# Loading the last unit's keys in two halves and splitting its exponential, in a streaming attention decode kernel on one Trainium2 core

## The chip, the cores and the metric

The kernel runs on one core of one Trainium2 chip. The metric is the device time of an execution in microseconds (us). Before the change it was 445.39 us in the median of four runs (444.75 to 446.24). The profile measures its span from the first to the last instruction, which is 1.7 to 3.2 us less. All runs quoted here were listed as fast (none took over 1.5% more than the fastest of its kernel), at a mean granted TensorE clock (the share of full speed that PE was given) of 0.93 to 0.97.

Three words for the trace. PE is TensorE, and "PEld" are its weight loads. DVE is VectorE and ACT is ScalarE. SP is the engine that issues the transfers.

## The reference, cut to what matters

Two attention decode layers, A and B, share one program. Each has 4 batches, one query token, 32 query heads on 8 key/value heads of 128, and a cache of 8192 positions. B looks only at the last 2048 positions.

```python
q = (x @ wq).reshape(B, Sq, Hq, Dh)...
scores = einsum("bhqd,bhkd->bhqk", q, k) * Dh ** -0.5
p = softmax(scores)
o = einsum("bhqk,bhkd->bhqd", p, v)
return o.reshape(B, Sq, Hq * Dh) @ wo          # A and B side by side
```

Some nine tenths of the 184.6 MB that are read are the two caches (estimate from their shapes, 168 MB), and every byte of them is used once.

## The kernel before

The work is cut into 20 units, four of B and sixteen of A. A unit of A is one batch and two key/value heads, with 4 MB of keys and 4 MB of values. Two units make a turn, and PE runs ten turns in a hardware loop. In a unit PE transposes the keys (16 groups k, through four PSUM banks), forms the scores of each group, and then multiplies the *previous* unit's probabilities with its values (eight chunks, "PV"). The last unit (L = 19) has its PV after the loop, in the tail:

```python
halves = [SA[(L + 1) % 2][0:Bn, 0:H2], KTB[2][0:Bn, 0:H2]]
def pe_seed(pe):                       # "the seed": brings the projection's running sum (f32) into PSUM, 4 matmuls in the trace
    for hf in range(2):
        ins = pe.matmul(out=halves[hf], lhsT=identf[0:Bn, 0:Bn], rhs=oacc[:, 0, ...], start=True, stop=False)
op("pe", pe_seed, waits=[("ocp", NTURN - 1), ("otr", L - 1)])
for c in range(NC):                    # the last unit's value chunks
    w = [("VL", vch_of[c])]            # its values land in four pieces
    if c == 0: w.append(("exp", L))
    if c == 4: pe_SM(L)                # sums of the probabilities
    pe_PV(L, c, bank=KTB[0], waits=w)
add_norm(L, bank=KTB[0])               # DVE scales the output
# ... then 16 matmuls of the last projection piece, whose weights land last
```

The loop's instructions carry fixed wait values, so at the end of each turn it takes back what the turn has used, one instruction per semaphore:

```python
with nc.Fori(0, n_turn, engines=[mybir.EngineType.PE]):
    run(turns[0])
    for n, sem in by_name.items():
        pe.sem_inc(sem, -strides[n])
```

## Time and profile before

| What | Reading before |
| --- | --- |
| time, median of 4 runs | 445.39 us |
| span of the profiled run | 442.5 us |
| moved | 184.78 MB at 418 GB/s |
| unit 18's keys let PE go | 396.57 |
| last unit's first transpose weights (T19) | 416.00 |
| last unit's output is scaled by DVE | 437.73, which is T19 + 21.73 |

From the page of the kernel before: the span, the row of the DMA engines' busy share in 40 slices (9 is 90% or more), and the chain of work that ended last.

```profile
span 442.5 us, 15650 instructions
DMA  8999999999999999999999999999999999999993
DMA packets 13047, 184.78 MB, mean 418 GB/s; under 512 B 1332, under 2 KB 2408, under 8 KB 4456
DMA 49%; PE 47%; issue 2%; SPq 1%; DVE 1%; ACT 0%
```

The transfers never pause until the last slice, so the bytes set most of the time. PE catches up with them once a pair of units and then waits. The timeline shows the last such wait, the place where the last unit begins, and the tail. Columns are start, duration, engine, line, operation, operands, count, and in brackets the engine's idle time before it and what ended it.

```profile
396.57 3.27 PEld L256 LDWEIGHTS KT<-identf,K_sb 128*128 128x128 f32 x16 [7.30 <-DMA K_sb<-in_A_k_cache_dram]
...
413.19 2.86 PEld L304 LDWEIGHTS OT<-PT,V_sb 128*128 128x128 bf16 x96
416.00 1.73 PEld L256 LDWEIGHTS KT<-identf,K_sb 128*128 128x128 f32 x16
...
430.17 0.69 DVE L434 TENSOR_TENSOR Dt<-SA,MBm 128x512 f32<-128x512 f32 x1
430.78 0.68 DVE L434 TENSOR_TENSOR Dt<-SB,MBm 128x512 f32<-128x512 f32 x1
431.49 1.06 ACT L443 ACTIVATE PT<-Dt 128x1024 bf16<-128x1024 f32 x1 [4.27 <-DVE Dt L434]
431.59 0.18 DVE L478 TENSOR_TENSOR OT_sb<-OS,RL 128x8 bf16<-128x8 f32 x1
432.33 0.11 PEld L642 LDWEIGHTS SA<-oacc,identf 4*4 4x4 f32 x2 [1.30 <-issue]
433.31 1.92 PEld L304 LDWEIGHTS KT<-PT,V_sb 128*128 128x128 bf16 x64 [0.43 <-issue]
437.73 0.18 DVE L471 TENSOR_TENSOR OT_sb<-KT,RL 128x8 bf16<-128x8 f32 x1 [1.21 <-PE KT L304]
```

Two things are to be seen. The last unit's transposes follow the 96 value matmuls before them with no idle bracket: PE came to them as it was done, and the keys, which landed at 415.96, held it back by no more than 0.02 us. It was almost a tie. And the seed (L642) starts 0.56 us after its input was ready (431.59 + 0.18 = 431.77) and 1.30 us after PE's last weight load, "issue", which means a wait for nothing that the profile counts.

What PE's sequencer did in that gap is only in the trace's own instruction records, which list the semaphore and branch instructions (start in us, duration, operation):

```
430.488 0.051 EVENT_SEMAPHORE $S[99]-=
430.672 0.051 EVENT_SEMAPHORE $S[122]-=
   (seven more, 0.151 apart)
431.877 0.051 EVENT_SEMAPHORE $S[101]-=
432.028 0.036 ALU_OP
432.124 0.076 COMPARE_BRANCH
432.259 0.051 EVENT_SEMAPHORE $S[130]>=
432.335 0.077 LDWEIGHTS (the seed's first)
```

Ten decrements and a branch close the loop. They start before the last value weights (430.936), because the sequencer runs ahead of the array, and end 1.2 us after them.

### The profile page before, as it was taken

The numbers are of one execution on the slowest core, as the hardware profiler recorded it, in microseconds if no ns is written. First come the engines' busy times: TensorE is split into PE (matmuls) and PEld (weight loads), VectorE is DVE, ScalarE is ACT, GpSimd is POOL, SyncE is SP. The second block draws the span as 40 slices with busy tenths as digits, with TensorE's granted clock in tenths as the row PEclk, the third lists the DMA queues.
The fourth block names the chain that finished last, engine by engine and source line by source line (L and its number), as shares of the span: only waits on it lengthen the run. The fifth ranks groups of instructions, "written<-read, shape, count | busy, mean of one in ns | idle before, by whom it ended". The sixth has DMA issues, their size and how long they took to land.

```text
span 442.5 us, 15650 instructions
## 1 busy us (share of the span) xinstructions
PE 359.4 (81%) x7282; PEld 336.2 (76%) x7282; DVE 209.8 (47%) x472; ACT 184.5 (42%) x183; POOL 21.3 (5%) x56
## 2 busy tenths in 40 slices
PE   0258898998995899399949984996799499939996
PEld 0248798898895889289948984896789498938995
DVE  0034455465473555256525652574356355525661
ACT  1004374474462437053615542553347143605541
POOL 6100000000000000000000000000000000000000
PEclk9999999999998899789979996999599979988999
DMA  8999999999999999999999999999999999999993
GB/s 335 424 416 424 417 418 421 421 455 398 455 402 449 429 429 424 436 435 429 427 438 435 427 427 424 429 416 444 435 429 425 431 442 432 424 427 429 432 401 107
DMA packets 13047, 184.78 MB, mean 418 GB/s; under 512 B 1332, under 2 KB 2408, under 8 KB 4456
## 3 DMA queue, kind: packets, MB, share of 16 engines
q1 hardware_dynamic: 12944, 184.56, 98.3%
q8 instruction: 8, 0.13, 0.1%
q14 instruction: 7, 0.06, 0.0%
q0 software_dynamic: 64, 0.02, 0.0%
q10 hardware_dynamic: 24, 0.01, 0.0%
HBM read 184.56 MB, written 0.01 MB: 417 GB/s over the span
## 4 chain that ended last, share of the span: by engine, by line
DMA 49%; PE 47%; issue 2%; SPq 1%; DVE 1%; ACT 0%
DMA K_sb<-in_A_k_cache_dram 43%; PE KT L256 28%; DMA K_sb<-in_B_k_cache_dram 7%; PE OT L304 5%; PE SA L289 4%; PE KT L367 4%; PE SB L289 3%; PE KT L304 1%; PE SA L316 1%; SPq L543 1%; PE KT L346 0%; PE KT L328 0%; PE SA L663 0%; PE KT L663 0%; DVE M L396 0%
## 5 line engine op out<-in xcount | busy, mean ns | idle before, releaser
L256 PE MATMUL KT<-identf,K_sb 128*128 128x128 f32 x1280 | 208.9, 298 | 55.9 <-DMA K_sb<-in_A_k_cache_dram 48.8
L265 ACT ACTIVATE KT_sb<-KT 128x1024 bf16<-128x1024 bf16 x160 | 162.3, 1022 | 144.4 <-PE KT L256 144.1
L256 PEld LDWEIGHTS KT<-identf,K_sb 128*128 128x128 f32 x1280 | 149.7, 151 | 63.7 <-DMA K_sb<-in_A_k_cache_dram 49.9
L264 DVE COPY KT_sb<-KT 128x512 int32<-128x512 int32 x160 | 110.3, 689 | 131.4 <-PE KT L256 130.1
L304 PE MATMUL OT<-PT,V_sb 128*128 128x64 bf16 x2560 | 84.4, 193 | 1.7 <-issue 1.7
L304 PEld LDWEIGHTS OT<-PT,V_sb 128*128 128x128 bf16 x2560 | 78.4, 98 | 1.8 <-issue 1.8
L289 PEld LDWEIGHTS SA<-RQc,KT_sb 128*128 128x128 bf16 x1280 | 56.5, 98 | 3.5 <-ACT KT_sb L265 1.0
L443 ACT ACTIVATE PT<-Dt 128x1024 bf16<-128x1024 f32 x20 | 21.1, 1057 | 86.3 <-DVE Dt L434 86.3
L289 PE MATMUL SA<-RQc,KT_sb 128*128 128x16 bf16 x1280 | 56.4, 170 | 0.0
L289 PE MATMUL SB<-RQc,KT_sb 128*128 128x16 bf16 x1280 | 55.6, 170 | 0.0
L289 PEld LDWEIGHTS SB<-RQc,KT_sb 128*128 128x128 bf16 x1280 | 51.6, 97 | 1.1
L396 DVE TENSOR_REDUCE M<-SB 128x8 f32<-128x512 f32 (+1 forms) x20 | 13.8, 692 | 43.4 <-PE SB L289 43.4
L417 POOL PARTITION_ALL_REDUCE MB<-M1m x20 | 7.7, 385 | 392.2 <-DVE M1m L410 392.2
L367 PE MATMUL KT<-Wo_sb,OL 128*4 128x512 bf16 x80 | 18.9, 379 | 0.0
L187 PE MATMUL KT<-ident,x_sb 4*128 4x4 bf16 x8 | 0.6, 170 | 19.2 <-POOL identf L505 19.2
L187 PEld LDWEIGHTS KT<-ident,x_sb 4*128 4x128 bf16 x8 | 0.4, 113 | 19.4 <-issue 19.4
L434 DVE TENSOR_TENSOR Dt<-SA,MBm 128x512 f32<-128x512 f32 x20 | 13.8, 692 | 0.7
L396 DVE TENSOR_REDUCE M<-SA 128x8 f32<-128x512 f32 (+1 forms) x20 | 13.6, 681 | 0.0
L434 DVE TENSOR_TENSOR Dt<-SB,MBm 128x512 f32<-128x512 f32 x20 | 13.6, 680 | 0.0
L316 PE MATMUL SA<-PT,onesb 128*128 128x64 bf16 x336 | 13.2, 192 | 0.0
L367 PEld LDWEIGHTS KT<-Wo_sb,OL 128*4 128x4 bf16 x80 | 6.0, 84 | 8.1
L316 PEld LDWEIGHTS SA<-PT,onesb 128*128 128x128 bf16 x336 | 11.1, 97 | 0.0
(68 smaller groups left out, 111.6 us busy)
## 6 DMA issues: line engine op xcount, KB each, us to landing
K_sb<-in_A_k_cache_dram SPq DMA_DIRECT2D x16, 4096.0 KB, 27.7
V_sb<-in_A_v_cache_dram SPq DMA_DIRECT2D x15, 4096.0 KB, 32.7
K_sb<-in_B_k_cache_dram SPq DMA_DIRECT2D x16, 1024.0 KB, 21.3
V_sb<-in_B_v_cache_dram SPq DMA_DIRECT2D x16, 1024.0 KB, 20.9
V_sb<-in_B_wq_dram SPq DMA_DIRECT2D x1, 4096.0 KB, 12.3
V_sb<-in_A_wq_dram SPq DMA_DIRECT2D x1, 4096.0 KB, 21.9
Wo_sb<-in_B_wo_dram SPq DMA_DIRECT2D x4, 1024.0 KB, 19.4
Wo_sb<-in_A_wo_dram SPq DMA_DIRECT2D x3, 1024.0 KB, 20.0
```

The lines of the kernel that those rows point to most:

```text
L256: ins = pe.transpose(out=bkf[:, pi * 128:(pi + 1) * 128], in_=K_sbf[:, slot, t0:t0 + 2, :].rearrange("p t d -> p (t d)"), identity=identf[ ...
L264: return e.tensor_copy(out=KT_sb.bitcast(I32)[:, tj % NKT, :], in_=bkf.bitcast(I32)[:, :])
L265: return e.activation(out=KT_sb[:, tj % NKT, :], in_=bk[:, :], func=ACTF.Copy)
L289: ins = pe.matmul(out=stb[:, t % NTH * C:(t % NTH + 2) * C], lhsT=ktv[:, pi, :, e], rhs=RQc[:, u % 2, t // TS, e, :], start=(e == 0), stop ...
L304: ins = pe.matmul(out=otb[:, s * NW:(s + 1) * NW], lhsT=V_sb[:, slot, t, :], rhs=PT[:, slot, t * C:t * C + NW], start=(j == 0), stop=(j == ...
L316: ins = pe.matmul(out=SA[u % 2][:, s * NW:(s + 1) * NW], lhsT=onesb[:, :], rhs=PT[:, u % 2, c0:c0 + NW], start=(i == 0), stop=(i == n - 1))
L367: ins = pe.matmul(out=bk[0:Bn, 0:D], lhsT=OL[:, i // REP, i % REP, :], rhs=Wo_sb[:, i // REP, i % REP, :], start=(i == 0), stop=(i == C - 1))
L396: return dve.tensor_reduce(out=M1[:, h * n:(h + 1) * n].rearrange("p (s h) -> p s h", h=C), in_=bank[:, :].rearrange("p (s j h) -> p s h j ...
L417: return pool.partition_all_reduce(MB[:, 0:n], M1m[:, 0:n], channels=128, reduce_op=ReduceOp.max)
L434: return dve.tensor_tensor(out=Dt[:, h * NTH * C:(h + 1) * NTH * C].rearrange("p (s j h) -> p s j h", s=Sh, h=C), in0=bank[:, :].rearrange ...
L443: return act.activation(out=PT[:, u % 2, 0:NT * C], in_=Dt[:, :], func=ACTF.Exp, scale=scale)
L543: return e.dma_start(out=dst, in_=src)
```

## The change

The intent was to give the tail earlier inputs. The last unit's keys come in two transfers, so that its first transposes need only half of them. The exponential comes in two halves, so that the first value chunks need only the first. The seed moves behind four value chunks, so that it no longer stands in front of them.

```diff
-            op("pe", fn, waits=[("K", u) if k == 0 else None, bankfree(idx)], ...)
+            op("pe", fn, waits=[("K", u) if k == 0 else ("KH", u) if k == NJ // 2 and u % 2 == 1 else None, bankfree(idx)], ...)
@@ value matmuls: those that would read past the first half are narrowed
+                    w = NW if bank is None or t >= NTH or t * C + NW <= NTH * C else C
@@ the last unit's exponential
-            add(act_exp(u))
+            if u == L:
+                add(act_exp(u, 0, 1))
+                add(act_exp(u, 1, 2))
+            else:
+                add(act_exp(u))
@@ tail
-        op("pe", pe_seed, waits=[("ocp", NTURN - 1), ("otr", L - 1)])
             if c == 0:
-                w.append(("exp", L))
+                w.append(("exp", L, 0))
             if c == 4:
                 pe_SM(L)
+                op("pe", pe_seed)
@@ loads; earlier odd units raise the new semaphore themselves, before their load
+            if kind == "K" and slot == 1 and u < L:
+                op("sp", lambda sp: sp.sem_inc(sems["kh"], 16), bump=(sems["kh"], 16, ("KH", u)))
+            if kind == "K" and u == L:
+                for h in range(2):
+                    ...  # 2 MB each, inc=("K", u, 0) and ("KH", u)
+                return
```

The loop body is shared by all turns, so the wait on the new semaphore, and its decrement at the loop's end, come in every turn.

## The prediction

> **What bounds the kernel now.** The page: span 442.5 us, 184.8 MB at 418 GB/s, the DMA row at 9 tenths almost throughout. The chain of waits is DMA 49%, PE 47%: each pair of units waits some 27 us for an even unit's keys. The last such wait ends at 396.57 (timeline, unit 18's keys). From there PE is hardly free: it starts the last unit's transposes at 416.003 and issues the loop's last matmul at 430.96. The bytes do not change, so only the time after 396.57 can shrink.
>
> **Part 1, keys in two halves.** The trace's semaphore records show the last key load completing engine by engine from 411.3 to 415.96 (the Trainium skill, "DMA: Bandwidth & Descriptors", why a DMA increments its semaphore by 16: the engines finish independently and the semaphore counts them; this trace agrees, 4.6 us apart). Half of the 4 MB is 5 us at the observed rate, so the first half should be complete near 411. But PE, in order, issued the previous unit's last value weights at 415.956 at their regular spacing of 0.029: it lost at most 0.02 us to this load. The early half only removes a near-tie, worth perhaps 0.1 us where PE runs faster.
>
> **Part 2, exponential in halves.** The subtractions end at 430.86 and 431.46; the exponential runs 431.49 to 432.55. A 4x256 activation took 0.37, so 512 elements should take about 0.6 (estimate): first half done near 431.5. Intended: value chunks begin then instead of at 433.31.
>
> I do not believe that. PE's sequencer is closing the loop, which the busy columns leave out: ten semaphore decrements 0.151 us apart, the last at 431.88, a branch at 432.12, the first instruction after the loop at 432.26, the seed's first weights at 432.335, though its input was ready at 431.77. Other loop ends look alike (idle 1.3 to 1.4 us, put down to "issue"). Nothing after the loop starts before 432.3, and the seed hid the exponential's end. With the seed moved, value chunks start near 432.5, and the seed's 0.98 us is paid later, before chunk 4. The PE work from loop end to last value matmul is unchanged: seed 0.98, chunks 1.86 and 1.9, sums 0.46.
>
> **Part 3, what is added.** The new key semaphore is waited on inside the loop, so each turn gets one more wait and one more decrement: 0.15 us at the exit, on the critical path, and up to 0.08 for the wait in the last unit, likely hidden. In earlier turns both lie in the 7 us wait for keys. Seven value matmuls narrow from 64 to 8 columns: at most 0.1 us saved.
>
> The value pieces land at 433.24, 434.65 and 435.84, the last weights at 438.45; PE needs them at 435.6, 436.6, 437.1 and 439.6: no wait, but no more than 1.1 us to win.
>
> **Sum.** +0.15 exit, up to +0.1 wait, up to -0.1 narrow matmuls, -0.1 near-tie: about +0.1. Predicted 445.6 us, range 444.4 to 446.7. Chances: faster by over 2% 0.01, within 2% 0.98, slower 0.01.
>
> **Right if** the last transposes still start near 416, a loop end has eleven decrements, the first value matmul comes 0.15 after the old seed start (0.8 sooner than before), the seed takes about 0.98 us before chunk 4, and the last normalisation starts 41.3 us after unit 18's keys (41.16 before). **Wrong if** value chunks start at 431.6 (the loop end is no gate: 0.7 us gain), if the moved seed costs much less than 0.98, or if two key transfers change the landing of the keys.

## The result, and the profile after

The changed kernel took 444.96 us in the median of four runs (444.10 to 445.62), beside 445.39 before. The ratio was 0.9988, with a 95% interval of 0.9964 to 1.0012. (A ratio is the mean time of one kernel's fast runs over that of the other's of the same rounds, so not quite the ratio of the medians.) The same kernel in five more runs on another occasion had 1.0015 (1.0001 to 1.0029). Where a run below is called slower or faster, the interval of its ratio excludes 1.

The profiled run of the changed kernel has a longer span than that of the kernel before, 443.6 against 442.5. Its page and its timeline at the places shown before:

```profile
span 443.6 us, 15670 instructions
DMA  8999999999999999999999999999999999999992
DMA packets 13191, 184.78 MB, mean 416 GB/s; under 512 B 1348, under 2 KB 2424, under 8 KB 4472
DMA 50%; PE 47%; issue 1%; SPq 1%; DVE 1%; ACT 0%
```

```profile
396.73 3.28 PEld L258 LDWEIGHTS KT<-identf,K_sb 128*128 128x128 f32 x16 [8.06 <-DMA K_sb<-in_A_k_cache_dram]
...
414.06 2.86 PEld L307 LDWEIGHTS OT<-PT,V_sb 128*128 128x128 bf16 x96
416.85 1.19 PEld L258 LDWEIGHTS KT<-identf,K_sb 128*128 128x128 f32 x11
...
431.77 1.23 ACT L448 ACTIVATE PT<-Dt 128x512 bf16<-128x512 f32 x2 [3.68 <-DVE Dt L437]
433.36 1.92 PEld L307 LDWEIGHTS KT<-PT,V_sb 128*128 128x128 bf16 x64 [1.45 <-issue]
435.79 0.09 PEld L652 LDWEIGHTS SA<-oacc,identf 4*4 4x4 f32 x2
436.74 1.92 PEld L307 LDWEIGHTS KT<-PT,V_sb 128*128 128x128 bf16 x64 [0.43 <-issue]
438.82 0.18 DVE L477 TENSOR_TENSOR OT_sb<-KT,RL 128x8 bf16<-128x8 f32 x1 [2.26 <-PE KT L307]
```

The chain of waits gets something wrong here that is worth knowing. It gives the place to the exponential:

```profile
431.77 1.23 ACT PT L448 x2
433.39 1.98 PE KT L307 x64
```

But the first value chunk needs only the first half, which ended at 432.40, almost a microsecond before. The instruction records show who it was: eleven decrements from 431.363 to 432.903, the branch at 433.151, and the first value weights at 433.361, in the same 0.21 us after the branch as the seed before.

Counted from T19, the tail reads like this (from the start times of the instruction records):

| After T19, us | before | after |
| --- | --- | --- |
| branch at the loop's end | 16.12 | 16.30 |
| first exponential half done | – | 15.55 |
| first value weights | 17.31 | 16.51 |
| seed | 16.33 | 18.93 |
| chunk 4 | 19.63 | 19.88 |
| output scaled by DVE | 21.73 | 21.97 |

The value chunks start 0.80 us sooner, as was meant, and the seed takes it all back before chunk 4. The tail is 0.24 us *longer*.

The rest of the longer span lies ahead of T19. From unit 18's keys to T19 PE took 19.43 us before and 20.12 after, on the same instructions. The table by stretches (stretch in us, its length, busy time and count per engine, granted PE clock, DMA share, GB/s) shows the cause, first for the kernel before, then for the changed one:

```profile
396.57:400.70 4.13, 4.12 (x26) 4.06 (x27) 1.47 (x3) 1.44 (x2) 0.00 (x0) 0.50 1.05 452
400.70:416.00 15.30, 15.30 (x325) 13.68 (x323) 9.04 (x21) 6.75 (x7) 0.37 (x1) 1.00 0.99 426
```

```profile
396.73:402.40 5.67, 5.67 (x40) 5.54 (x41) 2.15 (x4) 2.05 (x2) 0.00 (x0) 0.50 0.96 413
402.50:416.80 14.30, 14.30 (x308) 12.71 (x307) 8.28 (x20) 6.14 (x6) 0.37 (x1) 1.00 1.02 435
```

After waiting for keys PE runs at half clock, for 4.1 us here and 5.7 us there. The Trainium skill ("TensorE: Matmul & The Clock Gate", Part 1, "What's actually happening") says that a free-running window of 3413 ns decides, so the point of release depends on where in it the work begins. This agrees: the half-clock stretches of these two traces last 6.8 or 10.2 us, two or three such windows, and end 4.1 and 5.8 us after the keys. I take it for the luck of a run and not for the change: the same stretch took 19.97 and 19.87 us in two later runs without split keys (e8_before_early, e13_half_seed). It is not shown, because the four traces with only the last unit's keys split, in the usual order, all had 19.61 to 20.17, and the five others without the split 19.43 to 19.48.

### The profile page after: what moved, and what is told of

Read it like the earlier page. It is cut to its first block, busy times and chain, and to the rows that moved or that the text cites. A ratio compares the mean times of both kernels' runs of the same rounds, so it can differ in the third digit from the quotient of the medians.

```text
span 443.6 us, 15670 instructions
## 1 busy us (share of the span) xinstructions
PE 358.4 (81%) x7282; PEld 335.3 (76%) x7282; DVE 210.0 (47%) x472; ACT 184.8 (42%) x184; POOL 21.4 (5%) x56
## 4 chain that ended last, share of the span: by engine, by line
DMA 50%; PE 47%; issue 1%; SPq 1%; DVE 1%; ACT 0%
DMA K_sb<-in_A_k_cache_dram 43%; PE KT L258 27%; DMA K_sb<-in_B_k_cache_dram 7%; PE OT L307 5%; PE SA L291 4%; PE KT L370 4%; PE SB L291 3%; PE KT L307 1%; PE SA L319 1%; SPq L549 1%; PE KT L349 0%; PE KT L331 0%; ACT PT L448 0%; PE SA L673 0%; PE KT L673 0%
## 5 line engine op out<-in xcount | busy, mean ns | idle before, releaser
L448 ACT ACTIVATE PT<-Dt 128x1024 bf16<-128x1024 f32 (+1 forms) x21 | 21.3, 1016 | 85.6 <-DVE Dt L437 85.6
```

Source lines behind the costliest of these rows:

```text
L448: return act.activation(out=PT[:, u % 2, a:b], in_=Dt[:, a:b], func=ACTF.Exp, scale=scale)
```

## The experiments

Two theories were open besides mine. *Mine*: the loop's end gates the tail, so the early exponential is of no use, and the new semaphore adds one decrement to it. *Rival 1*: the early half of the keys pays whenever PE is early. *Rival 2*: the split exponential pays. The times of a whole run scatter by up to 2 us, in part for the reason above, so the theories are separated by the time from T19 to the scaled output, which repeats to 0.04 us between two profiles of the changed kernel (21.97 and 21.93). Part of the scatter lies outside the profile's span, which is 1.7 us shorter than the time in some runs and 3.2 in others. Runs are named by their labels.

### The change again, and its two parts

The first run is the changed kernel itself:

> The changed kernel unaltered, timed in more rounds. My theory (the loop's end gates the tail): ratio to the kernel before 0.999 to 1.0005; in its trace eleven decrements at the last loop end, the first value weights 16.4 to 16.6 us after the last unit's first transpose weights (before: seed 16.33, first value weights 17.31), the normalisation 21.97 after them (before 21.73). Rival 1 (the early first half of the keys pays whenever PE reaches the last unit before its keys): ratio 0.998 to 0.999, and in fast-clock executions the last unit starts earlier than the whole keys could have landed. Rival 2 (the split exponential pays): ratio 0.997 or less with the first value weights no more than 15.8 after the first transpose.

The keys alone (the value matmuls have their 64 columns again, too):

```diff
-                add(act_exp(u, 0, 1)); add(act_exp(u, 1, 2))
+            add(act_exp(u))
+        op("pe", pe_seed, waits=[("ocp", NTURN - 1), ("otr", L - 1)])
-                w.append(("exp", L, 0))
+                w.append(("exp", L))
```

> Keys in two halves with the new semaphore, exponential whole and seed first as before. My theory: the loop end costs one decrement more (0.15 us), so from the last unit's first transpose to the normalisation about 21.9 us (before 21.73), ratio 0.999 to 1.001. Rival 1: this part alone brings what the whole change brings, ratio 0.998 to 0.999. Rival 2: no gain, ratio 1.000 or above.

The exponential and the seed alone, with no new semaphore:

```diff
-waits=[("K", u) if k == 0 else ("KH", u) if k == NJ // 2 and u % 2 == 1 else None, bankfree(idx)]
+waits=[("K", u) if k == 0 else None, bankfree(idx)]
-            if kind == "K" and slot == 1 and u < L: ...
-            if kind == "K" and u == L: ...
```

> Exponential in two halves and the seed moved, keys whole and no new semaphore. My theory: ten decrements; first value weights at the place where the seed began before, 16.33 us after the last unit's first transpose; normalisation at 21.7 to 21.85; ratio 0.9995 to 1.0005. Rival 2: first value weights 15.6 to 15.8 after it, normalisation near 21.0, ratio about 0.998.

| Run | median us | ratio (95%) | decrements | first value weights, after T19 | scaled output, after T19 |
| --- | --- | --- | --- | --- | --- |
| before | 445.18 (9 runs) | 1 | 10 | 17.31 | 21.73 |
| e1_after | 445.83 | 1.0015 (1.0001 to 1.0029) | 11 | 16.47 | 21.93 |
| e2_keys_only | 445.57 | 0.9996 (0.9982 to 1.0010) | 11 | 17.49 | 21.90 |
| e3_exp_only | 444.59 | 0.9985 (0.9971 to 0.9998) | 10 | 16.36 | 21.81 |

In the tail the parts add up. Counted from T19 the keys cost 0.18 us, the exponential and the seed 0.09, and together they cost 0.21 to 0.24. Of each, 0.02 is not theirs. In the trace of the kernel before, the keys held T19 itself back by 0.018 us, and PE made this up by the last transpose, which came 9.77 us after T19. It came 9.79 to 9.80 after it wherever T19 was not held back, with the new wait in the body (after, e1, e2) and without it (e3, e8, e13), so this wait cost nothing measurable. Counted from the loop's last value weights, the tail is 6.79 us before, 6.94 with the keys alone, 6.86 with the exponential and the seed alone, and 7.01 with all (6.98 in e1_after). So the keys cost one decrement, 0.15 us, and the exponential and the seed 0.06.

The first value weights of e3_exp_only come where the seed stood before, 16.36 against 16.33, after the same idle time of 1.30 us, which is what the gate of the loop's end demands. Rival 2 fell: it wanted 15.6 to 15.8.

```profile
432.55 1.92 PEld L307 LDWEIGHTS KT<-PT,V_sb 128*128 128x128 bf16 x64 [1.30 <-issue]
```

The ratios do not add up (0.9996 and 0.9985 beside 1.0015). e3_exp_only came out a little below what I expected, near the 0.998 of rival 2, and e1_after a little above, and their intervals do not overlap. The tail explains little of it. Of the 1.24 us between the spans of their two traces 0.12 lies in the tail, 0.69 in the stretch from unit 18's keys to T19, and 0.42 in the landing of unit 18's keys. I read the last two as the scatter of the clock windows and of the landings. That is argued for those runs, since only one of each was traced.

### What the whole keys cost without the split

Every kernel here with whole keys in the usual order shows how long PE waited for them, as the gap between its last value weights and T19 beyond the usual 0.029 us. Seven traces had 0.018 (before), 0 (e3_exp_only), 0.285 (e4_before_peeled), 0.039 (e7_exp_early), 0 (e8_before_early), 0.119 (e12_early_seed) and 0 (e13_half_seed), mean 0.07. The three longest belong to runs whose half clock ended soonest, 3.4 to 4.1 us after unit 18's keys. In all four traces with a wait T19 came 0.04 us after the landing of its keys, and 19.43 us after unit 18's first transpose, which is the spacing of the two landings (396.53 and 415.96 in the kernel before). PE made up as much as 0.09 us of a wait by the last transpose, so the loss that reaches the tail is smaller, 0.2 us in e4_before_peeled and 0.03 in the mean. So rival 1 has its mechanism right and a size of at most 0.3 us at T19, 0.07 in the mean, beside a cost of 0.15.

To see the split where the keys do gate, two runs put the last key load behind unit 18's value load, a wrong order on purpose:

```diff
-            if u < NU:
+            if u < L:
                 kv_load("K", u)
             kv_load("V", u - 1)
+            if u == L:
+                kv_load("K", u)
```

> The kernel before with its last key load queued behind unit 18's value load, so that the last unit's keys land about 9.8 us later (near 425.8) and gate. My theory: the last unit starts at 425.8, PE idles about 9.8 us before it and then runs some 3.4 to 6.8 us at half clock; span 10 to 13 us longer than before, ratio 1.022 to 1.03. It is a wrong order on purpose, to make the keys the gate.

> The keys-in-halves variant with the same late order. My theory: where the keys gate, the split is worth most of half a load: first half lands near 421, the last unit starts there, its second half is gated at 425.8, and the span is 4 to 6 us shorter than the run before (ratio to the kernel before 1.010 to 1.016). If the split brought nothing even here, both late runs agree within 1 us.

They took 456.93 us (ratio 1.0254, 1.0229 to 1.0279) with whole keys and 451.85 us (1.0135, 1.0111 to 1.0160) with halves, both as expected. PE's timeline at T19, whole first, halves second:

```profile
426.20 3.67 PE L256 MATMUL KT<-identf,K_sb 128*128 128x128 f32 x16 [9.40 <-DMA K_sb<-in_A_k_cache_dram]
```

```profile
420.98 3.56 PE L258 MATMUL KT<-identf,K_sb 128*128 128x128 f32 x16 [4.91 <-DMA K_sb<-in_A_k_cache_dram]
```

The same split that is worth 0.07 us or less in the real order is worth 5.1 us here. The idea is sound. It was put where PE did not wait.

### Splitting where PE does wait

PE waits for the keys of the even units, so another run splits all of A's:

```diff
-... ("KH", u) if k == NJ // 2 and u % 2 == 1 else None
+... ("KH", u) if k == NJ // 2 and u % 2 in (0, 1) else None
-            if kind == "K" and u == L:
+            if kind == "K" and slot in (0, 1):
```

> The changed kernel with every A unit's keys in two halves (one more semaphore, for even units). In the change only the last unit was split, where PE came late anyway; here the split is also where PE waits, at the even units. My theory: unit 18 starts near 391.8 instead of 396.6, its second half is gated by the second landing near 396.6; the last unit starts near its first half's landing at 411.3 to 412 and ends its value work before 427; then the pieces of values gate (landing 430.7 to 435.9) and the last weights at 438.4: the first value weights near 430.8, the normalisation near 436.4, the last projection matmul right after 438.4; span 1.0 to 1.2 us shorter than before, ratio about 0.9975, if the half-speed clock after idling does not fall into the tail. Rival: all transfers are one queue and the DMA time is the bound, so nothing moves, ratio 0.9995 to 1.0005.

It took 446.32 us, ratio 1.0027 (1.0006 to 1.0049): slower, against both expectations. PE's idle times in its timeline:

```profile
407.39 0.64 PE L307 MATMUL OT<-PT,V_sb 128*128 128x64 bf16 x16 [1.07 <-DMA V_sb<-in_A_v_cache_dram]
412.28 1.97 PE L258 MATMUL KT<-identf,K_sb 128*128 128x128 f32 x16 [0.58 <-DMA K_sb<-in_A_k_cache_dram]
426.88 0.74 PE L307 MATMUL OT<-PT,V_sb 128*128 128x64 bf16 x16 [3.47 <-DMA V_sb<-in_A_v_cache_dram]
434.05 1.98 PE L307 MATMUL KT<-PT,V_sb 128*128 128x64 bf16 x64 [1.48 <-issue]
```

The keys came early, T19 moved from 416.0 to 412.3, and then PE stood 3.5 us before unit 18's *values*. I had left out that wait: before, those values landed at 425.69 and PE wanted them at about 426.9. Here they landed at 426.84, and loop end and tail followed from there. The later landing has a pattern. From the landing of one odd unit's values to the next, each of six turns took 0.13 to 0.18 us longer than before (41.55 instead of 41.41, for one), so each pair of split loads cost about 0.15 us of transfer time. What in the transfers costs that was not tried.

### Is the loop's end the gate?

First, more of the suspected cost: ten more additions and subtractions at each loop end, on the changed kernel.

```diff
                 for n, sem in by_name.items():
                     pe.sem_inc(sem, -strides[n])
+                for r in range(5):
+                    pe.sem_inc(sems["kh"], 16)
+                    pe.sem_inc(sems["kh"], -16)
```

> The changed kernel with ten more semaphore additions and subtractions at each loop end, on a semaphore that does not change in sum. My theory: each costs 0.151 us on PE's sequencer and at the last loop end all of it is on the critical path: first value weights 1.5 us later after the last unit's first transpose (16.5 becomes 18.0), normalisation 23.45 to 23.5 (21.95 in the changed kernel), ratio about 1.0035 to 1.005; in the earlier turns the wait for keys swallows it. If the sequencer's additions run beside the matmuls, nothing moves.

The first value weights came at T19 + 18.01, the expected 18.0. The run was slower than expected, 449.66 us, ratio 1.0094 (1.0058 to 1.0130), and the output was scaled at 26.48 instead of 23.5. PE's idle time and the granted clock after it say why:

```profile
434.53 2.57 PE L307 MATMUL KT<-PT,V_sb 128*128 128x64 bf16 x64 [2.87 <-issue]
```

```profile
431.60:434.50 2.90, 0.06 (x3) 0.00 (x1) 0.64 (x3) 1.02 (x2) 0.00 (x0) 1.00 0.97 330
435.50:442.40 6.90, 6.90 (x109) 5.35 (x105) 0.63 (x2) 0.00 (x0) 0.00 (x0) 0.51 0.04 12
```

An idle time of 2.9 us at the loop's end was followed by half clock for most of the tail. The usual 1.3 to 1.5 us, in the kernel before and the changed one, were not.

Second, the loop's end moved out of the way, by writing the last turn out after the loop:

```diff
-            with nc.Fori(0, n_turn, engines=[mybir.EngineType.PE]):
+            with nc.Fori(0, n_turn - 1, engines=[mybir.EngineType.PE]):
...
-                taken[n] += strides[n] * n_turn
+                taken[n] += strides[n] * (n_turn - 1)
+            run(turns[-1])
```

> The kernel before, with the last turn of PE's loop written out after the loop: the decrements and the branch fall into the wait for unit 18's keys. My theory: no decrements at the tail; the seed starts when its input is ready (about 0.1 after the last unscaled output is normalised), 15.9 us after the last unit's first transpose instead of 16.33; then value weights follow the whole exponential or the seed, whichever ends last, near 16.85, and the normalisation is at about 21.3 instead of 21.73: 0.4 us gained, ratio 0.999. If something else than the loop's end held the seed (a semaphore, the switch to 4-row weights), the seed stays at 16.33 and nothing is gained. Risk: [...]a stall of 1 to 2 us like the one at 55.4 us in the kernel before may appear.

It took 447.50 us, ratio 1.0049 (1.0035 to 1.0062), slower. The decrements were gone from the tail, but the named risk came true:

```profile
432.13 0.77 PE L304 MATMUL OT<-PT,V_sb 128*128 128x64 bf16 x21 [1.26 <-issue]
...
434.45 3.58 PE L304 MATMUL KT<-PT,V_sb 128*128 128x64 bf16 x64
```

PE stopped for 1.26 us between two value matmuls that waited for no semaphore, and after a further idle time of 0.59 us before the seed the next chunks ran 3.58 us instead of 2, at half clock:

```profile
434.50:437.90 3.40, 3.40 (x67) 3.40 (x67) 0.00 (x0) 0.00 (x0) 0.00 (x0) 0.50 0.27 94
```

The Trainium skill ("Runtime: NRT & Kernel Launch", "Instruction fetch mechanics") says that instructions are streamed sequentially at mostly hidden cost, and counsels unrolling because a taken branch can stall. In the kernel before, PE was idle for 1.29 and 1.24 us at the two loop ends that did not meet a wait for keys, beside 1.21 at the exit where no branch is taken. So a taken branch cost some 0.1 us at most, and the code written out had a stall of 1.26. The kernel before has one like it, 1.7 us, in its first pass through the loop. A stall of fetching is my guess, since the trace names no cause.

Third, the decrements that are long over are made earlier. Six of ten go into the last unit's body, at least six steps after the last wait on their semaphore; four stay. The distance matters, because the sequencer runs ahead of PE: the decrements at the loop's end began 0.45 us before the last weights. This was done to the exponential-only variant and to the kernel before:

```diff
-                run(turns[0])
-                for n, sem in by_name.items():
-                    pe.sem_inc(sem, -strides[n])
+                # one decrement after each of the scores 4 to 11 of the odd unit,
+                # if at least 6 steps after the last wait on that semaphore
+                run(turns[0], drop)
+                for n in rest:          # the evictions' two, the exponential's, one value semaphore
+                    pe.sem_inc(by_name[n], -strides[n])
```

> The exponential-only variant (split exponential, seed moved, whole keys, no new semaphore), with six of the ten decrements moved from the loop's end into the last unit's transposes, well after the last wait on each. My theory: four decrements stay at the end, so the loop ends 0.9 us sooner; now the first exponential half gates: first value weights about 15.6 us after the last unit's first transpose weights (16.36 in the exponential-only variant), normalisation near 21.05 (21.81 there, 21.73 before): about 0.7 us gained on the kernel before, ratio 0.9985. If the decrements in the body cost PE what they cost at the end, the loop's last value weights come 0.9 us later (14.95 becomes 15.8) and nothing is gained.

> The kernel before with the same six decrements moved. My theory: the seed is now gated by its input, 15.9 us after the last unit's first transpose (16.33 before), value weights at 16.9 (whole exponential ends near 16.55, hidden behind the seed), normalisation near 21.3: 0.4 us gained, ratio about 0.999. The split of the exponential is then worth the difference to the previous run, about 0.25 us. If the loop's end was not the gate, the seed stays at 16.33.

| Run | median us | ratio (95%) | branch | first value weights | scaled output, all after T19 |
| --- | --- | --- | --- | --- | --- |
| e7_exp_early | 444.43 | 0.9978 (0.9960 to 0.9996) | 15.17 | 15.62 | 21.08 |
| e8_before_early | 445.01 | 0.9988 (0.9968 to 1.0008) | 15.21 | 16.88 | 21.30 |

All four times from T19 met the expectation within 0.05 us. The loop's end moved 0.9 us forward, the six decrements in the body cost nothing (last value weights of the loop at 14.91 and 14.96, before 14.93), and now the inputs gate. In e8_before_early PE's idle time before the seed is 0.85 us instead of 1.30. In e7_exp_early PE waits for the first exponential half, as the change had intended:

```profile
431.72 1.98 PE L307 MATMUL KT<-PT,V_sb 128*128 128x64 bf16 x64 [0.51 <-ACT PT L448]
```

So the split exponential with the moved seed is worth 0.22 us (21.30 less 21.08) once the gate is away. Counted from the loop's last value weights it is 0.18, since the keys held T19 back in e7_exp_early, and it costs 0.06 while the gate stands.

### A version that beats both

With the gate away, PE has idle time in front of the first exponential half, and the seed can begin in it if it waits only for what it needs. That is the reciprocal of unit 18's sums (after it nobody reads that bank), not unit 18's scaled output:

```diff
-                op("pe", pe_seed)                       # before chunk 4
+        op("pe", pe_seed, waits=[("ocp", NTURN - 1), ("rcp", L - 1)])   # first in the tail
```

> Exponential in halves, six decrements moved into the body, and the seed first again, but waiting for the reciprocal of unit 18's sums instead of unit 18's normalised output. It then fills the time in which the first exponential half is still running. My theory: seed about 15.4 us after the last unit's first transpose, first value weights at 16.4, normalisation at about 20.8 (21.08 with the seed before chunk 4, 21.73 in the kernel before); ratio about 0.998. If the seed still delays the tail as much as before chunk 4, normalisation stays at 21.08.

And half of the seed can go: DVE adds the running sum in its final copy, and only ACT's half is seeded.

```diff
-            for hf in range(2):
+            for hf in range(1, 2):
...
-dve.tensor_copy(out=osb[:, 0, 0:H2], in_=halves[0])
+dve.tensor_tensor(out=osb[:, 0, 0:H2], in0=halves[0], in1=oacc[:, 0, 0:H2], op=AluOpType.add)
```

> The run before with half the seed: only the half that ScalarE copies out is seeded; VectorE adds the running sum to the other half in its final copy. My theory: two of four seed matmuls go, first value weights gated by the first exponential half at 15.6 to 16.0, normalisation near 20.3 to 20.4; VectorE's last operation stays near 0.41 us; the last projection matmul then waits for the last weights' landing (22.3 to 22.5 after the first transpose) or just misses it; 1.0 to 1.3 us gained on the kernel before, ratio 0.997 to 0.9975. If VectorE's addition costs far more than the copy, the gain shrinks by that.

| Run | median us | ratio (95%) | seed | first value weights | scaled output, all after T19 |
| --- | --- | --- | --- | --- | --- |
| e12_early_seed | 444.07 | 0.9971 (0.9950 to 0.9992) | 15.33 | 16.31 | 20.70 |
| e13_half_seed | 443.52 | 0.9955 (0.9937 to 0.9973) | 15.42 | 15.97 | 20.35 |

DVE's last operation is as short as the copy was, 0.41 us:

```profile
439.52 0.41 DVE L677 TENSOR_TENSOR osb<-SA,oacc 4x256 bf16<-4x256 f32 x1 [1.98 <-PE SA L673]
```

In both runs the seed starts 0.21 us after the branch, so the rest of the loop's end gates it again, and the first value weights follow the seed and not the first exponential half, which was done at 15.45 and 15.54.

e13_half_seed is faster than both kernels: its tail is 1.37 us shorter than before, and its six runs (443.12 to 443.95) all lie below the fastest of the twelve of before beside them (444.59). Its ratio is below the expected 0.997 to 0.9975: the medians differ by 1.88 us, and what makes up the rest beside the tail is not shown. Little more is left there. In its trace the last weights landed at 438.77, and the last projection matmul, which needs them, loaded its weights at 439.21.

## Why the prediction was right or wrong

The time was right: predicted 445.6 (444.4 to 446.7) and within 2%, measured 444.96, and 445.83 in the later runs. That tests little, since the unchanged 445.39 lies in the range too. The mechanism is tested by its points:

- **"PE, in order, ... lost at most 0.02 us to this load": right for that trace, and the first half landed at 411.29 as predicted.** The near-tie, "worth perhaps 0.1 us", measured 0 to 0.285 us, mean 0.07, in seven traces. Two transfers did change the landing of the keys, which the prediction names under "wrong if", but by little: the second half landed 19.50 us after unit 18's keys, the whole load 19.43.
- **"Nothing after the loop starts before 432.3": right.** The branch, not an input, released the tail in both kernels. Ten more additions and subtractions moved the first value weights by 1.50 us, and six decrements fewer at the end made the tail wait for its inputs.
- **"First half done near 431.5": right.** It ended 15.55 us after T19, which is 431.55 on the clock of the kernel before. The half took 0.63 us (estimate 0.6).
- **"+0.15 exit, up to +0.1 wait": right for the exit,** 0.15 measured in e2_keys_only. The wait cost nothing measurable.
- **"The seed's 0.98 us is paid later": mis-sized by 0.09.** In its new place the seed delays chunk 4 by 1.06 us: from the sums to the next chunk it is 1.53 instead of 0.47.
- **"Up to -0.1 narrow matmuls": nothing came of it.** The first four chunks took 1.82 us with 64 columns and 1.82 with seven matmuls of 8.
- **"The last normalisation starts 41.3 us after unit 18's keys": wrong.** It was 42.09. The step that failed is the starting point: I took PE's stretch from unit 18's keys to T19 as fixed at 19.43 us, and a longer half clock made it 20.12. (19.43 was the spacing of the two key landings, with which PE tied in that trace, and PE alone can need more.) From T19 the tail was 21.97 us, where the predicted parts give 21.73 + 0.15 to 0.25.

The sign of the whole difference stays unresolved. The tail is 0.24 us longer, 0.22 counted from the loop's last value weights, the avoided wait gives back less than 0.1 in the mean, and the runs gave 0.9988 and 1.0015. Whether the split has a part in the longer half clock is open. Also open are the stall in the written-out turn and the transfer time that split loads cost.

## What to carry to other kernels

Before feeding a tail earlier inputs, look at what the engine's sequencer does in front of it: semaphore bookkeeping and branches show in no busy column, and a chain of waits then blames the last input although it was there long before. A split transfer is worth up to half a load where the engine waits for it and nothing where it comes late, so read the wait at that very place, and then the next wait behind it, first. When run times scatter by more than the effect, measure from a mark behind the source of the scatter to a mark behind the effect.

## What the Trainium skill lacked or had wrong

- No page has the cost of a semaphore decrement that PE's sequencer makes by itself. Here it is 0.151 us each when they follow one another, so ten of them with a branch leave PE idle for 1.3 us, while six placed among transposes and scores cost nothing measurable.
- "Runtime: NRT & Kernel Launch", "Instruction fetch mechanics", counsels unrolling. Here PE was idle for 1.24 and 1.29 us at two loop ends with a taken branch and for 1.21 at the exit, and the written-out last turn stopped for 1.26 us in straight code and took 447.50 us against 445.18.
- "TensorE: Matmul & The Clock Gate", Part 1, was borne out in its window. It gives the run-to-run spread of the transition as plus or minus 0.5 us. Here the spread was wider: the end of the half clock lay 3.4 to 5.9 us after unit 18's keys in thirteen traces of this kernel's variants.
- "DMA: Bandwidth & Descriptors", "Why a DMA increments its semaphore by 16 and not by 1", says that the engines finish independently. It gives no size. Here the first and the last engine's increments of one 4 MB load lay 4.6 us apart.
